# Two k transposes as paired row tiles, and a new order of steps and loads, in an attention and token-MLP kernel

## The chip, the cores and the metric

One core of one Trainium2 chip. The metric is the device time of one execution in microseconds (us). Before: 114.95 us, the median of 3 runs (114.75 to 115.07). The *span* of a run, which the traces show, is about 2 us shorter than its time.

## The reference

Two attentions after each other (32 packed queries p against k and v, then q against what that gives), and on their output a token-mixing MLP with relu:

```python
# batch 8, heads 8, seq 576, head_dim 64, 32 packed queries; float32 in and out
p_packed = softmax_attn(p, k, v)                # (8, 8, 32, 64)
x = softmax_attn(q, p_packed, p_packed)         # (8, 8, 576, 64) -> (8, 576, 512)
W_tok = (1 / 8) * einsum('bsd,btd->bst', x @ w_q, x @ w_k)      # w_q, w_k: (512, 64)
out = relu(einsum('bst,btd->bsd', W_tok, x)) @ w_out            # w_out: (512, 512)
```

## The kernel before

The kernel is written as one long list of steps, `ORDER`, that a loop turns into instructions one by one; no scheduler moves them. `KT.7.0=4` is step KT (transposes of k), batch 7, part 0, into PSUM bank 4; `@A`, `@V` and `@P` name ScalarE (ACT), VectorE (DVE) and GpSimd (POOL). In this kernel a bank has one user at a time: whoever fills it next waits until its last content was copied out.

The steps that matter here: LD loads k, q or v of a batch; KT and QT transpose them and KE and QE copy the result out of PSUM; S1 and PV are the first attention; RS, RR and AM are the sum, reciprocal and product of the second softmax, AT transposes its result; GM, Y and MX are the matmuls of the token mixing, RL its relu, and YE copies the result of Y; OT is the last matmul, OE copies its result into an output buffer, and a full buffer is stored. In the first 26 us, WARM are matmuls whose result nobody uses, and PX transposes p.

```python
opool = ctx.enter_context(tc.tile_pool(name="opool", bufs=9))      # output buffers: nine pairs
psum = ctx.enter_context(tc.tile_pool(name="psum", bufs=1, space=bass.MemoryType.PSUM))

def bank(n, shape, dt, name):
    return psum.tile(shape, dt, tag=f"bank{n}", name=name)

KROW, MROW = (), range(8)              # KROW: the batches with k in row tiles

def KT(b, c, eng, bk):
    if b in KROW and c == 0:           # already there, unused in before
        src = k_in[b].rearrange("a u n -> a (u n)")
        T["kt", b, c] = [bank(n, [P, 16, 64], bf16, "kT_ps") for n in bk]       # two banks
        for n, m in enumerate(KM[0] + KM[1]):
            for i in range(2):         # rows 0-63 and 64-127 in turn
                nc.tensor.transpose(T["kt", b, c][i][:, n], src[halves(i), m * P:(m + 1) * P],
                                    idb[halves(i), halves(i)])
        return
    ...                                # else: 128x128 transposes, eight to a bank

def OE(b, t, *a):                      # copy a result into its half of an output pair
    ...
    o = new("o", (b, tp), [P, 2, D], fp32, "o", opool)
    copy(eng, o[:, t % 2, x:x + w], T["ot", b, t, x])
    done[b, tp] = done.get((b, tp), 0) + w
    if done[b, tp] == 2 * D:
        store(o.rearrange("a e n -> a (e n)"), b, tp * 8, 2)        # two DMAs of 256 KB

def put(dst, o):
    if last: held.append(nc.sync.dma_start(dst, o))
    else:    held.append((dst, o))     # stores are held back ...

def release(load):                     # ... until the last load in ORDER has landed
    last.append(load)
    for n, (dst, o) in enumerate(held):
        i = nc.sync.dma_start(dst, o)
        if n == 0:
            tc.add_manual_dep(i.ins, load.ins.name, ...)            # wait for that load
```

The softmax here doesn't subtract the row's maximum and nothing guards it: scores larger than these inputs give would overflow.

## Time and profile before

| | before |
|---|---|
| median time | 114.95 us |
| span of the profiled run | 112.9 us |
| TensorE busy | 103.7 us (92%) |
| ACT, DVE, POOL busy | 74%, 65%, 34% |
| last load landed | 78.20 us |
| first two stores: issued, landed | 78.29 and 78.99, 81.21 and 81.89 us |
| TensorE's last matmul ends | 107.50 us |

TensorE is busy in nearly every slice. Its share says little about single waits, so the view to start from is the waits of TensorE (line of the waiting instruction, what ended the wait, total us, times, longest us). Three entries are all that before has:

```profile
PE warm_ps L603 <- DVE warm L138: 1.5, 1, 1.5
PE kT_ps L298 <- DMA k_sb<-in_k_dram: 0.9, 1, 0.9
PE pv_ps L340 <- ACT e L328: 0.6, 1, 0.6
```

The first is the start of the program, the last lies at 13.8 us in the first batch. Between them stands the one wait that a change can remove, for k of batch 7. What these lists don't show are instructions that run slowly; for that I use an *offset*: the start of a step in the trace, minus the sum of the undisturbed durations of all matmuls ahead of it in `ORDER`. An offset that stays level means that TensorE runs at its own pace; each step up is a wait or a slow stretch.

### The profile page before, as it was taken

Reading aid. Unit: us, or ns where it says so; the run is one execution under the profiler, and the core shown is the slowest. Engines: PE = TensorE matmul, PEld = TensorE weight load, DVE = VectorE, ACT = ScalarE, POOL = GpSimd, SP = SyncE. Lnnn points to the kernel's source line nnn. Section 1 sums busy time; section 2 is a strip of 40 time slices with the busy share of each in tenths; the row PEclk is TensorE's granted clock in tenths of the full one; section 3 lists DMA queues with packets and bytes.
Section 4 is the critical chain, followed back from the end, with each engine's and each line's share of the span. In section 5 each row is a group of like instructions: output and inputs, shape, how many; then the busy total and the mean of one; then the engine's idle time right before and its main releaser. Section 6 shows DMA issues by size and latency. Waiting matters only on the chain.

```text
span 112.9 us, 4280 instructions
## 1 busy us (share of the span) xinstructions
PE 103.7 (92%) x1842; PEld 73.3 (65%) x1855; DVE 73.5 (65%) x186; ACT 83.0 (74%) x169; POOL 38.3 (34%) x49
## 2 busy tenths in 40 slices
PE   4999799999999999999999999699999999999900
PEld 2458768688767758797848876594985664644500
DVE  2066776947988667795959895669688484916300
ACT  0026859998996875998989676687999989958420
POOL 6972206962550000585490390040008053000000
PEclk9999999999999999999999999999999999999996
DMA  3999999999999999999999999991889999994893
GB/s 83 379 202 206 208 190 209 208 207 211 204 217 203 212 209 211 209 208 211 209 209 209 214 207 208 205 175 26 256 282 312 305 334 338 319 333 148 291 316 135
DMA packets 16035, 25.44 MB, mean 225 GB/s; under 512 B 2656, under 2 KB 10848, under 8 KB 16016
## 3 DMA queue, kind: packets, MB, share of 16 engines
q0 software_dynamic: 11792, 14.42, 73.6%
q1 hardware_dynamic: 3872, 9.90, 26.6%
q10 hardware_dynamic: 352, 0.85, 2.3%
q8 instruction: 14, 0.23, 0.8%
q14 instruction: 5, 0.04, 0.1%
HBM read 30.15 MB, written 9.44 MB: 351 GB/s over the span
## 4 chain that ended last, share of the span: by engine, by line
PE 70%; DMA 12%; ACT 7%; DVE 2%; issue 2%; POOL 1%
PE out_ps L536 22%; DMA k_sb<-in_k_dram 12%; PE warm_ps L603 7%; PE kT_ps L298 6%; PE qT_ps L386 6%; PE pv_ps L340 5%; PE aT_ps L440 4%; PE e_ps L322 4%; PE wkq_ps L461 3%; PE mix_ps L504 3%; PE e_ps L405 3%; ACT kT L131 2%; PE wkq_ps L456 2%; PE g_ps L478 2%; ACT e L414 1%
## 5 line engine op out<-in xcount | busy, mean ns | idle before, releaser
L431 POOL TENSOR_TENSOR a<-e,rr 128x512 bf16<-128x512 f32 (+1 forms) x13 | 16.1, 1245 | 45.1 <-DVE rr L425 21.6
L536 PE MATMUL out_ps<-wout,relu 128*128 128x512 bf16 (+1 forms) x120 | 30.6, 373 | 0.6
L131 ACT ACTIVATE o<-out_ps 128x512 f32<-128x512 f32 (+1 forms) x26 | 15.4, 590 | 7.7 <-PE out_ps L536 7.4
L536 PEld LDWEIGHTS <-relu 128*128 128x128 bf16 x132 | 11.8, 98 | 10.1 <-issue 0.3
L421 DVE TENSOR_REDUCE rs<-e 128x16 f32<-128x512 f32 (+1 forms) x16 | 12.9, 809 | 3.2 <-ACT e L414 3.0
L514 ACT ACTIVATE relu<-mix_ps 128x512 bf16<-128x512 f32 x21 | 11.5, 607 | 1.4 <-PE pv_ps L340 1.2
L414 ACT ACTIVATE e<-e_ps 128x512 f32<-128x512 f32 (+1 forms) x24 | 11.7, 530 | 0.7 <-PE e_ps L405 0.5
L603 PE MATMUL warm_ps<-warm 128*128 128x512 f32 (+1 forms) x24 | 10.8, 580 | 1.5 <-DVE warm L138 1.5
L131 ACT ACTIVATE qT<-qT_ps 128x1024 bf16<-128x1024 bf16 (+1 forms) x12 | 9.8, 831 | 2.4 <-PE qT_ps L386 2.4
L328 ACT ACTIVATE e<-e_ps 128x512 bf16<-128x512 f32 (+1 forms) x24 | 11.2, 502 | 0.2 <-PE e_ps L322 0.2
L386 PE MATMUL qT_ps<-idb,q_sb 128*64 128x128 bf16 x288 | 10.9, 220 | 0.0
L298 PE MATMUL kT_ps<-idb,k_sb 128*128 128x128 bf16 x126 | 9.9, 220 | 0.9 <-DMA k_sb<-in_k_dram 0.9
L386 PEld LDWEIGHTS <-q_sb 128*64 128x64 bf16 x288 | 8.8, 110 | 0.7 <-issue 0.3
L135 DVE COPY kT<-kT_ps 128x1024 bf16<-128x1024 bf16 (+1 forms) x14 | 7.8, 566 | 2.0 <-PE kT_ps L298 2.0
L516 DVE TENSOR_SCALAR relu<-mix_ps 128x512 bf16<-128x512 f32 x11 | 7.3, 687 | 2.6 <-PE mix_ps L504 2.0
L298 PEld LDWEIGHTS <-k_sb 128*128 128x128 bf16 x126 | 7.5, 98 | 2.2 <-DMA k_sb<-in_k_dram 1.1
L340 PE MATMUL pv_ps<-v_sb,e 64*64 64x192 bf16 x288 | 8.4, 244 | 0.6 <-ACT e L328 0.6
L182 POOL DMA_DIRECT2D k_sb<-in_k_dram x7 | 5.3, 761 | 7.6 <-PE ppT_ps L356 3.1
L461 PE MATMUL wkq_ps<-aT,pqk 128*128 128x256 bf16 (+1 forms) x64 | 7.9, 233 | 0.0
L135 DVE COPY o<-out_ps 128x512 f32<-128x512 f32 (+1 forms) x7 | 4.6, 654 | 4.7 <-PE out_ps L536 3.6
L322 PE MATMUL e_ps<-pdiag,kT 128*64 128x64 bf16 x288 | 7.4, 197 | 0.0
L440 PE MATMUL aT_ps<-idb,a 128*128 128x128 bf16 x80 | 7.1, 220 | 0.2
(81 smaller groups left out, 193.3 us busy)
## 6 DMA issues: line engine op xcount, KB each, us to landing
out_dram<-o SPq DMA_DIRECT2D x31, 256.0 KB, 3.8
q_sb<-in_q_dram POOLq DMA_DIRECT2D x8, 576.0 KB, 13.8
v_sb<-in_v_dram POOLq DMA_DIRECT2D x8, 576.0 KB, 12.6
k_sb<-in_k_dram POOLq DMA_DIRECT2D x7, 576.0 KB, 13.0
out_dram<-o_rem SPq DMA_DIRECT2D x4, 256.0 KB, 4.1
k_sb<-in_k_dram ACTq DMA_DIRECT2D x1, 576.0 KB, 3.6
k_sb<-in_k_dram SPq DMA_DIRECT2D x1, 576.0 KB, 5.0
wout<-in_moe_w_out_dram POOLq DMA_DIRECT2D x2, 256.0 KB, 13.0
```

The source lines that it names most:

```text
L131: nc.scalar.activation(o, i, COPY)
L135: nc.vector.tensor_copy(o, i)
L298: nc.tensor.transpose(ps[:, n], src[:, o:o + P], idb if b else idf)
L322: nc.tensor.matmul(ps[halves(i), at[0]:at[1] + 1:at[1] - at[0]], T["kT", b][:, place(b, m), halves(i)], rhs, start=True, stop=True)
L340: nc.tensor.matmul(T["pv", b][i][halves(cc)], lhsT, rhs, start=n == 0, stop=n == R - 1, skip_group_check=True)
L386: nc.tensor.transpose(o[halves(x)], q_in[b][:, x, r * Dh:(r + 1) * Dh], idb)
L414: nc.scalar.activation(e2(b, min(c, 1))[:, o:o + n], T["s2", b, c].rearrange("a t i c (x l) -> a (t i c x) l", l=L), EXP, scale=scale)
L421: e.tensor_reduce(rs, T["e2", (b, d)], axis=AX, op=ADD)
L431: e.tensor_tensor(a2[:, 2 * d:2 * d + n].rearrange("a t i (u l) -> a (t i u) l", l=L), T["e2", (b, d)], T["rr", (b, d)].to_broadcast((P, n ...
L440: nc.tensor.transpose(ps[:, i, t - 2 * c], T["a2", b][:, t, i], idb)
L536: nc.tensor.matmul(ps, lhsT, wout[:, j, x:x + w], start=j == 0, stop=j == NJ - 1)
L603: nc.tensor.matmul(ps[:, 0:n], warm[:, 0:P], warm[:, 0:n], start=True, stop=True)
```

## The change

Two things: k of batches 6 and 7 goes through two row tiles at once (32 transposes of 64 rows in place of 16 of 128), and all steps and loads have a new order. The intent: shorter transposes, and k of batch 7 needed later, so that its load isn't waited for. Nearly all of the diff is `ORDER`; its core:

```diff
-    KROW, MROW = (), range(8)
+    KROW, MROW = (6, 7), range(8)
...                                     # start, loads k7 and k6, end (excerpts)
-LD.p0 LD.K0 LD.K1 LD.p1 LD.P SET.warm@V LD.q0 SET.aT1@V WARM.0=0 SET.idf@V LD.v0 SET.aff@P
-KT.0.0=1 KT.0.1=2 WARM.1=3 PX.0=4 LD.k1 KT.0.3=5 KT.0.4=6 KE.0.0@V KE.0.1@V LD.W SET.pd0@V
+LD.p0 LD.K0 LD.K1 LD.p1 SET.warm@V WARM.5=0 SET.idf@V LD.P WARM.0=1 SET.aff@P PX.0=2 WARM.9=3
+WARM.7=4 SET.pd0@V KT.0.4=5 KT.0.1=6 KE.0.1@A KT.0.3=7 LD.q0 SET.v0@V SET.mask@V KT.0.2=0
...
+KT.6.0=6,0 MR.3=3 PP.5.1@V OT.3.2=2 AE.4.1@V PT.5=5 OT.3.3=4 AE.4.0@A WKQ.4.0=1 OE.3.2@A
...
-KE.7.0@A AE.5.1@V X2.6.1@A KT.7.2=6 WKQ.5.0=5 S2.6.0=1 WKQ.5.1=4 WR.5@V KT.7.1=0 S1.7.0=3 WE.5.0@A
-QT.7.1=2 KE.7.2@V X2.6.0@A QT.7.0=6 X2.6.2@A S1.7.2=5 KE.7.1@V RS.6.0@V RS.6.1@V QT.7.2=1 X1.7.0@A
-WE.5.1@A S1.7.1=7 QE.7.0@A QK.6=0 QKE.6@V GM.5=3 OT.4.1=4 X1.7.1@A GE.5@A Y.5=6 RR.6.0@V X1.7.2@A
+QE.6.1@V AT.5.1=5 AE.5.2@A AE.5.1@V KT.7.0=4,6 PT.6=7 AT.5.0=0 PE.6@V KT.7.1=3 AE.5.0@V KE.7.1@A
+WKQ.5.1=1 WKQ.5.2=2 S2.6.1=5 S2.6.2=7 WKQ.5.0=0 X2.6.2@A OT.4.3=3 MR.4=7 WR.5@V KE.7.0.1@V
+WE.5.0@V WE.5.1@A KE.7.0.0@V X2.6.1@A GM.5=2 S2.6.0=6 OE.4.3@A S1.7.0=1 X2.6.0@A GE.5@V S1.7.2=0
+QK.6=5 QT.7.2=4 QT.7.1=3 RS.6.1@V S1.7.1=2 RS.6.0@V X1.7.2@A X1.7.0@A QKE.6@A QT.7.0=6 Y.5=0
...
```

The loads end, in before, with k6 v5 q6 q7 k7 v6 v7, and after with q6 v5 k6 q7 v6 k7 v7.

## The prediction

Some clauses are cut from it, and marked; none of them is a term of its sum, which comes to 113.8 us, put at 113.7, from durations and offsets in the trace of before.

> **What bounds the kernel now.** I read the page first (engine shares, slices), then the chain of waits in order of time, then TensorE's timeline, then the issues and landings of the loads.
>
> ```profile
> PE 103.7 (92%) x1842; PEld 73.3 (65%) x1855; DVE 73.5 (65%) x186; ACT 83.0 (74%) x169; POOL 38.3 (34%) x49
> PE   4999799999999999999999999699999999999900
> PEclk9999999999999999999999999999999999999996
> DMA  3999999999999999999999999991889999994893
> GB/s 83 379 202 206 208 190 209 208 207 211 204 217 203 212 209 211 209 208 211 209 209 209 214 207 208 205 175 26 256 282 312 305 334 338 319 333 148 291 316 135
> ```
>
> TensorE is full in nearly every slice, at the full clock; the others stand at 34 to 74%. The transfers run at a steady 205 to 215 GB/s up to slice 26 (76 us): these are the loads. From slice 28 on the stores follow, held back by the kernel until the last load has landed. So there are two belts beside each other: TensorE, and the loads. Which leads is seen in the chain and the timeline:
>
> ```profile
> 57.05 1.43 POOL a L431
> 58.48 14.07 DMA k_sb<-in_k_dram
> 72.59 0.62 PE kT_ps L298 x8
> ...
> 105.60 1.91 PE out_ps L536 x12
> 107.53 0.60 ACT o L131
> ```
>
> ```profile
> 50.76 1.03 PE L536 MATMUL out_ps<-wout,relu 128*128 128x512 bf16 x3
> 51.62 0.40 PE L478 MATMUL g_ps<-wkq,a 128*128 128x64 bf16 x8
> 51.85 0.22 PE L478 MATMUL g_ps<-wr,a 128*128 128x64 bf16 x2
> 51.91 1.17 PE L298 MATMUL kT_ps<-idb,k_sb 128*128 128x128 bf16 x18
> 52.92 0.28 PE L405 MATMUL e_ps<-ppT,qT 128*128 128x64 bf16 x4
> ...
> 72.59 0.62 PE L298 MATMUL kT_ps<-idb,k_sb 128*128 128x128 bf16 x8 [0.94 <-DMA k_sb<-in_k_dram]
> 73.14 0.30 PE L488 MATMUL y_ps<-pp,g 64*64 64x128 bf16 x4
> 73.37 0.44 PE L322 MATMUL e_ps<-pdiag,kT 128*64 128x64 bf16 x16
> ```
>
> The 14 us of "DMA" in the chain are k of batch 7, issued at 58.48 and landed at 72.55; all that time TensorE worked on other things, and only 0.94 us of idle TensorE came of it. Its last matmul ends at 107.5, an eviction (0.60) and the last stores make 112.9. From start to start the timeline gives the true rate: 18 transposes in 1.01 us are 56 ns each; the block at 72.59 takes 0.55 where 8 x 56 = 0.45, so a change of tiling mode (128x128 to 64x64) costs about 0.10, and over all such places 0.094.
>
> With such numbers for each kind of step (0.864 for four 512-column matmuls, 29 ns for 64 columns, 15.6 ns for the paired half-array ones of L322, 28 ns for L386, 79 for four of L340) I added up all matmuls in the order of before: 99.35 us. The place of each step in the trace is this sum plus an offset that only waits raise: 1.46 (start), +1.85 (cold first matmuls: the first four take 3.6 us, later ones half), 5.4 at 28 us, 5.9 at 40, 6.4 at 65 (small waits in the first batches, and drift), +1.10 at the k of batch 7, 8.0 at the end. So half the waiting is in the first 26 us, and later there is one wait worth naming.
>
> [...]half-array pairs come 31 ns a pair for 64 columns, and a mode change costs 94 ns. [...]the changed kernel gives each row tile its own bank. [...]before has 29 ns for 64 columns, and 15.6 where two tiles alternate[...]. [...]here all bf16 loads come from POOL on one queue, and before shows them land one by one, one per 2.83 us (589,824 B / 2.83 us = 208 GB/s[...]).
>
> **The change part by part.**
>
> Row tiles. For batches 6 and 7, 16 of 18 transposes of 128x128 become 32 of 64 rows, each moving 64 columns, two alternating in two row tiles and banks. If they pair as L322's column tiles do: 32 x 15.6 = 0.50 us against 16 x 56 = 0.90; 0.40 saved a batch, 0.80 in all. Evictions: still two of 1,024 columns and one of 256 a batch (0.68 on DVE, 1.02 on ACT), but with 64-element runs in the output, and the scores of a batch now need both. They come microseconds later; no cost. Each block adds two changes of mode (4 x 0.094 = 0.38), but the new order saves as many: I counted 56 changes in both kernels. Warm-up matmuls are the same ten. So TensorE's sum falls from 99.35 to 98.55.
>
> Order. k of batch 7 is now wanted much later: 71.1 in the new sum, 65.1 in the old. That wait goes (1.10). But the loads too stand in another order, and k of batch 6 has gone from seventh to fifth of the loads counted from the end. I put the loads in the landing slots of before (k4 46.05, ... v5 63.02, then 66.35, 69.03, 72.55, 75.36, 78.20) and compared with where the new sum wants them. The offset needed so that no step waits: k2 5.2, k3 5.5, q2 5.7, v3 5.9, q3 6.1, v4 6.4, v5 6.3, k6 6.8, k7 only 4.3, v7 1.3. Before's own offset there is 5.2 to 6.4. So the new order runs TensorE right along the belt of loads from 26 to 66 us, and k of batch 6 (slot 66.35, wanted at 59.55 + 6.4 = 65.95) costs some 0.4. After it nothing waits on a load.
>
> Sum. TensorE starts k of batch 6 at 66.4. Left in the new sum: 39.0 (row tiles counted). Drift as in before from there to the end, without the k7 wait: 0.46. For new small waits I add 0.35: near the end all four relus of batch 7 stand on DVE (4 x 0.69 = 2.75 us, against some 2.9 us of matmuls before the first that needs the last of them), and batch 6's y is evicted behind an output copy. That gives 106.2 for the last start, against 107.34: 1.1 us less. The tail (last eviction, last stores, 5.4) is built the same. Stores: after 79.6 us they need about 0.8 us per 256 KB, and before has the queue empty at 102 to 103.5; they can end about a microsecond sooner, hardly two. So span 112.9 - 1.1 = 111.8, and with the 2.05 by which time and span differ, 113.8. A little of the chance lies lower (no wait for k6, no small waits), so I say 113.7.
>
> **The rivals.**
>
> 1. The loads still set the end. For: the slots are tight at k6, and a PE that gains before 66 us gains nothing. Against: the stall needs only 0.4. If q6's slot (3.3 us, a slow one in before) was slow by chance, k6 lands at 65.9 and the time is 113.3. If the loads slip, for instance because POOL issues one late behind a multiply that waits for DVE, as it did at 45 us, each microsecond is one in the end: 114.7.
>
> 2. Row tiles don't pair[...]. Before has no such case; its 48-row transposes in one row tile (33 in 1.25 us with four mode changes) take some 26 ns each. 32 x 26 = 0.83: nearly nothing saved, and the time is 114.4. Only batches 6 and 7, those behind the last tight load, have the change; saving in the earlier ones would gain nothing by the argument above, so this choice fits with a true saving.
>
> 3. The stores bind the end. They need 36 x 0.8 = 28.6 from 79.6, that is 108.2 if never short of data, and the last ones run until 111.5. With TensorE 1.1 sooner there is still slack; with 2 there would not be. This caps the gain at about 2 us, 113.0.
>
> 4. The first batches wait more. The first transposes start later (tally 4.2 against 1.7), but the belt of loads takes up any offset to 6.8, so up to a microsecond costs nothing.
>
> **Range and chances.** The centre is 113.7. Everything well (no k6 wait, no new waits): 112.9. No pairing and half a microsecond of new waits: 114.8. 2% faster is 112.65, and needs more than row tiles, the k7 wait and the k6 slot together give: 0.08. 2% slower is 117.25 and needs a stall of 3 us that nothing points to: 0.02. Within 2%: 0.90.
>
> **What would show it.** Right: the transposes of L298 in batches 6 and 7 start 15 to 16 ns apart, 0.50 us a block; no wait of TensorE for k of batch 7; a wait of 0.2 to 0.6 for k of batch 6 near 66 us; landings still 2.83 apart and the last near 78.2; TensorE's end near 106.3; the tail 5.4. Wrong: starts 25 ns apart or more; the last load later than 79; waits of TensorE for ACT or DVE of over 0.5 us in the last 40 us; store slices full up to the end with the last eviction long done.

## The result, and the profile after

After: 116.65 us, the median of 4 runs (116.31 to 118.25); before in the same rounds 114.92 (114.75 to 115.07). The ratio of the fast runs is 1.0141, with a 95% interval of 1.011 to 1.0172. Ratios here are the mean time of one kernel's fast runs over the mean of the other's of the same rounds, so not quite the ratio of the medians. Executions over 1.5% slower than the fastest of the same kernel are left out of the means. I had predicted 113.7 with 112.9 to 114.8: a gain of 1.2 us where there is a loss of 1.7.

The profiled run was a slow one (118.25 us), so what follows is checked below in a fast one. The page's slices, engine TensorE and moved GB/s:

```profile
PE   4999999999999999999999979999969997999800
GB/s 85 375 201 205 188 212 207 209 207 208 210 209 206 209 213 210 210 211 208 213 205 208 215 203 210 206 85 50 206 310 321 307 334 344 302 201 289 287 266 87
```

From 14 us on, TensorE's slices were full in before but for one (the wait for k of batch 7); now one at 66 us, one at 84 and one at 95 are not. The waits of TensorE name all three:

```profile
PE qT_ps L386 <- ACT o L131: 1.2, 1, 1.2
PE kT_ps L290 <- DMA k_sb<-in_k_dram: 0.7, 1, 0.7
PE aT_ps L440 <- POOL a L431: 0.4, 1, 0.4
PE aT_ps L440 <- DVE a L431: 0.2, 1, 0.2
```

And TensorE's timeline (start us, busy us, line, tiles, shapes, count, and in brackets the idle time and what ended it):

```profile
67.08 0.64 PE L290 MATMUL kT_ps<-idb,k_sb 64*128 64x64 bf16 x32 [0.66 <-DMA k_sb<-in_k_dram]
67.65 0.29 PE L509 MATMUL mr_ps<-wr,y 128*128 128x128 bf16 x2
...
80.97 1.03 PE L536 MATMUL out_ps<-wout,relu 128*128 128x512 bf16 x4
...
84.52 0.64 PE L386 MATMUL qT_ps<-idb,q_sb 128*64 128x128 bf16 x16 [1.16 <-ACT o L131]
...
96.19 0.40 PE L440 MATMUL aT_ps<-idb,a 128*128 128x128 bf16 x4 [0.40 <-POOL a L431]
```

The row tiles do as predicted: 67.08 to 67.65 is 0.57 us, of which one mode change takes 0.094 (as in before); 32 transposes in 0.48 are 15 ns each, against 0.90 us for the sixteen of before. The wait for k of batch 7 is gone. But the step at 84.52, QT.7.1, waits 1.16 us for an output copy on ACT. That copy is OE.4.3, of the bank that the OT at 80.97 had begun to fill 3.5 us before. Why it came so late is in the chain of waits (start us, us, what):

```profile
75.79 2.71 PE out_ps L536 x12
78.52 0.60 ACT o L131
79.44 4.33 DMA out_dram<-o
83.88 0.60 ACT o L131
84.52 0.64 PE qT_ps L386 x16
```

and ACT's timeline shows the copy itself waiting for a store:

```profile
83.88 0.60 ACT L131 ACTIVATE o<-out_ps 128x512 f32<-128x512 f32 x1 [1.72 <-DMA out_dram<-o]
```

Read from the bottom: QT.7.1 needs bank 3; bank 3 is free when OE.4.3 has copied it out; OE.4.3 opens the *tenth* output pair (batch 4, tiles 2 and 3), and there are nine buffers; so it waits for the first pair to be stored; no store may start until the last load has landed (78.66), so the first two were issued at 78.74 and 79.44, and they landed at 83.16 and 83.77. In before the tenth pair's first copy came later: OT.4.1 of the tenth pair came on TensorE at 84.5, its copy at 85.3, without a wait, and the first pair had landed at 81.89. From before's timelines of TensorE and ACT:

```profile
84.47 0.81 PE L536 MATMUL out_ps<-wout,relu 128*128 128x512 bf16 x3
85.32 0.60 ACT L131 ACTIVATE o<-out_ps 128x512 f32<-128x512 f32 x1
```

There is a second part: these stores took 4.4 us where those of before took 2.9. The trace of the DMA packets shows a cause by its time, not by name. One instruction transfer of 16 KB (the profile's queue 8, "instruction") runs from 80.0 to 81.7 us, and right behind it the stores stand nearly still. This is the DMA view of 78 to 86 us, in slices of 0.2 us; the four low ones are 81.8 to 82.6 us:

```profile
GB/s 0 0 0 0 0 0 0 0 0 0 287 225 143 246 328 369 307 287 307 62 20 20 20 184 225 225 205 369 410 348 307 379 348 379 399 256 184 266 184 287
```

In three of the four 20 GB/s flow, against 287 to 369 in the microsecond before. What holds the stores there is not shown.

In before that transfer came at 82.2, when two stores had landed and the third was about to (82.66); the fourth took 5.2 us. Part of that is its place in the queue: in a later run of before's order (k of batch 7 loaded earlier) the transfer came only at 83.9, and the fourth store took 3.9 us without it.

Where the time went, in offsets (us) at five places. The fast run is the first experiment below:

| offset of TensorE at | predicted | after (slow run) | after (fast run) |
|---|---|---|---|
| the row tiles of batch 6 | 6.8 | 7.5 | 7.4 |
| 84 us, before QT.7.1 | | 7.7 | 7.5 |
| 88 us | | 9.4 | 9.3 |
| 98 us, behind AT.7 and MX.6 | | 10.4 | 10.3 |
| the end | 7.6 | 10.4 | 10.4 |
| last matmul ends | 106.3 us | 109.12 us | 109.11 us |

The sum of matmuls is 98.55 us in all three columns. The end is 2.8 us later than predicted and the time 2.95 us longer.

### The profile page after: what moved, and what is told of

Same layout as the page of the kernel before. It is cut to its first block, busy times and chain, and to the rows that moved or that the text cites. A ratio compares the mean times of both kernels' runs of the same rounds, so it can differ in the third digit from the quotient of the medians.

```text
span 115.2 us, 4349 instructions
## 1 busy us (share of the span) xinstructions
PE 104.9 (91%) x1887; PEld 72.6 (63%) x1887; DVE 81.2 (70%) x200; ACT 75.0 (65%) x158; POOL 34.5 (30%) x46
## 4 chain that ended last, share of the span: by engine, by line
PE 67%; DMA 13%; ACT 7%; DVE 4%; issue 3%; POOLq 1%; POOL 0%; SPq 0%; ACTq 0%; DVEq 0%
PE out_ps L536 20%; PE warm_ps L603 9%; DMA k_sb<-in_k_dram 9%; PE kT_ps L298 6%; PE qT_ps L386 5%; PE pv_ps L340 5%; DMA out_dram<-o 4%; PE e_ps L322 4%; PE e_ps L405 3%; PE mix_ps L504 2%; PE wkq_ps L461 2%; PE aT_ps L440 2%; ACT o L131 2%; ACT relu L514 1%; DVE rs L421 1%
## 5 line engine op out<-in xcount | busy, mean ns | idle before, releaser
L431 POOL TENSOR_TENSOR a<-e,rr 128x512 bf16<-128x512 f32 (+1 forms) x10 | 12.3, 1237 | 51.0 <-DVE rr L425 24.5
L131 ACT ACTIVATE o<-out_ps 128x512 f32<-128x512 f32 (+1 forms) x30 | 17.8, 595 | 11.6 <-PE out_ps L536 9.2
L536 PEld LDWEIGHTS <-relu 128*128 128x128 bf16 x132 | 11.5, 98 | 11.3 <-issue 1.9
L603 PE MATMUL warm_ps<-warm 128*128 128x256 f32 (+1 forms) x24 | 11.6, 611 | 1.5 <-DVE warm L138 1.5
L516 DVE TENSOR_SCALAR relu<-mix_ps 128x512 bf16<-128x512 f32 x17 | 11.2, 681 | 1.0 <-PE mix_ps L504 0.9
L514 ACT ACTIVATE relu<-mix_ps 128x512 bf16<-128x512 f32 x15 | 8.1, 596 | 3.7 <-issue 1.4
L131 ACT ACTIVATE kT<-kT_ps 128x256 bf16<-128x256 bf16 (+2 forms) x7 | 4.5, 638 | 7.3 <-PE kT_ps L298 7.3
L135 DVE COPY qT<-qT_ps 128x1024 bf16<-128x1024 bf16 (+1 forms) x14 | 8.2, 589 | 1.2 <-PE qT_ps L386 1.2
L135 DVE COPY aT<-aT_ps 128x512 bf16<-128x512 bf16 (+1 forms) x17 | 5.9, 357 | 3.0 <-PE aT_ps L440 3.0
L298 PE MATMUL kT_ps<-idb,k_sb 128*128 128x128 bf16 x94 | 7.4, 219 | 0.0
L322 PEld LDWEIGHTS <-kT 128*64 128x64 bf16 x288 | 6.4, 112 | 1.5 <-DVE rr L425 0.8
```

The source lines that it names most:

```text
L131: nc.scalar.activation(o, i, COPY)
L135: nc.vector.tensor_copy(o, i)
L298: nc.tensor.transpose(ps[:, n], src[:, o:o + P], idb if b else idf)
L322: nc.tensor.matmul(ps[halves(i), at[0]:at[1] + 1:at[1] - at[0]], T["kT", b][:, place(b, m), halves(i)], rhs, start=True, stop=True)
L431: e.tensor_tensor(a2[:, 2 * d:2 * d + n].rearrange("a t i (u l) -> a (t i u) l", l=L), T["e2", (b, d)], T["rr", (b, d)].to_broadcast((P, n ...
L536: nc.tensor.matmul(ps, lhsT, wout[:, j, x:x + w], start=j == 0, stop=j == NJ - 1)
```

## The experiments

Sixteen kernels, all correct. Kernels of one heading group ran on the same chip beside the same runs of before: 115.45 us (median of 11 runs) for the first four (chip 3), 115.08 for the second (chip 9), 115.15 for the third (chip 2) and 114.99 for the last (chip 9 again). The theory from the traces (A): nine output buffers are too few for this order, and the copy of the tenth pair waits for the first stores. Rivals: B, the wait belongs to the slow profiled run; C, the loss is in the stores' rate, whoever waits; D, the row tiles themselves harm.

### First four: the unchanged kernel, the buffers, the release, the row tiles

**The changed kernel again.** No edit.

> The changed kernel once more, unaltered, for a profile in the usual state (the first one was 118.25 us against 116.3 to 116.8 of its fast runs). Theory A (a tenth output pair finds no free output buffer, because all stores wait for the last load): ACT again waits about 1.5 us on the landing of a store ahead of an output copy near 82 us, and TensorE over 1 us for it. Rival B (that wait belongs to the slow profile only): no such wait, and the fast time of 116.5 comes from elsewhere. Time 116.2 to 116.9 either way.

Measured: 116.60 us, ratio 1.0118 (1.0075 to 1.016), and the profile fell in a fast run. The waits of TensorE in it (further entries left out):

```profile
PE qT_ps L386 <- ACT o L131: 1.3, 1, 1.3
...
PE aT_ps L440 <- POOL a L431: 0.4, 1, 0.4
```

The first two stores landed 4.28 and 4.19 us after issue, and an instruction transfer stood at 80.0 us. B falls.

**Ten output buffers.** The room comes from a second pool.

```diff
-    opool = ctx.enter_context(tc.tile_pool(name="opool", bufs=9))
+    opool = ctx.enter_context(tc.tile_pool(name="opool", bufs=10))
-            o = opool.tile([P, D], fp32, tag="orem", name="o_rem", bufs=4)
+            o = opool.tile([P, D], fp32, tag="orem", name="o_rem", bufs=2)
```

> The changed kernel with ten output buffers instead of nine (the room comes from the remainder buffers, two instead of four). Theory A: ACT's wait on a store near 82 us is gone, TensorE's 1.2 us wait behind it too; and if the two later waits (0.3 and 0.6 us near 95 us, for the attention weights of batch 7) are its followers, those as well: 114.3 to 115.3. Rival C (the stores' belt sets the end whatever TensorE does): TensorE ends sooner but the time stays at 116.2 or more. Rival B: no change, 116.5.

Measured: 115.25 us, ratio 0.9987 (0.9942 to 1.0032). The two longest waits of TensorE behind its start:

```profile
PE aT_ps L440 <- POOL a L431: 0.4, 1, 0.4
PE px_ps L257 <- DMA p<-in_p_dram: 0.3, 1, 0.3
```

The wait at QT.7.1 is gone, and the offset after 84 us rises by 0.2 in place of 1.8. The stores are nearly as slow as without the edit (4.03 us, an instruction transfer at 79.8): it is the buffer that makes their slowness matter. The time falls by 1.35 us against the changed kernel on the same chip. TensorE's end is at 107.00. A is confirmed, and it isn't the whole miss: the kernel is now level with before, not 1.2 us faster, and 0.9 us of waits at AT.7 and MX.6 stay.

**Nine buffers, stores released when k of batch 7 has landed.** One load earlier.

```diff
-        end = [item for item in ORDER.split() if item.startswith("LD.")][-1]
+        end = "LD.k7"
```

> The changed kernel with the stores let go when k of batch 7 has landed, one load (2.8 us) before the last. Theory A: the first pair's stores land near 81 us instead of 83.8, the tenth pair finds its buffer, TensorE's wait near 83 us is gone: 114.5 to 115.5, and the tail may gain as the stores start earlier. Rival C: the stores' belt sets the end, and starting it 2.8 us earlier gains nearly that: 113.5 to 114.5, below what ten buffers give. Against both: the stores slow the last load; v of batch 7 is wanted at 85.9 us and has slack of 7.

Measured: 115.44 us, ratio 0.9997 (0.9953 to 1.004). The first stores are issued at 74.94 and land at 78.78; the wait at QT.7.1 is gone too, and TensorE ends at 107.00, as with ten buffers. An earlier start of all stores gains nothing beyond the freed buffer, so nothing speaks for C.

**The new order without row tiles.** Three transposing steps of k in batches 6 and 7 as in before, in the places of the new order.

```diff
-    KROW, MROW = (6, 7), range(8)
+    KROW, MROW = (), range(8)
-KT.6.0=6,0 MR.3=3 ... KT.6.1=6 ...
+KT.6.0=6 KT.6.1=0 MR.3=3 ... KT.6.2=6 ...
-... KT.7.0=4,6 PT.6=7 ... KT.7.1=3 ...
+... KT.7.0=4 KT.7.1=6 PT.6=7 ... KT.7.2=3 ...
```

> The changed kernel's order with the k of batches 6 and 7 transposed as before (18 full transposes, no row tiles). TensorE's sum rises by 0.8 us less two pairs of mode changes of 0.19 each, so 0.4. If that lies on the path behind the k of batch 6: 116.9. If theory A holds and part of TensorE's saving is eaten by the wait for the buffer near 82 us (which ends when the store lands, not when TensorE comes), only the batch 7 half counts: 116.6 to 116.8. If row tiles harm (second eviction needed before the scores): below 116.4.

Measured: 115.84 us, ratio 1.0052 (1.0003 to 1.0101): 0.8 us faster than with the row tiles by the medians, though the runs overlap (115.25 to 116.90 against 116.39 to 117.53). The first stores landed 2.91 us after issue (78.01 to 80.92), the instruction transfer came at 82.3, and TensorE had no wait at QT.7.1, still with nine buffers (shorter waits and those of the first batch left out):

```profile
PE kT_ps L298 <- DMA k_sb<-in_k_dram: 0.5, 1, 0.5
PE aT_ps L440 <- POOL a L431: 0.4, 1, 0.4
```

So row tiles and wait are tied together, and not through TensorE's own time, which the row tiles shorten, nor through the harm that the expectation names (D, a second copy before the scores): in the fast run with row tiles no wait of TensorE for the copies KE is listed. They add 64 TensorE instructions (each transpose with its weights is two), and with them the instruction transfer falls 2.3 us earlier, on the first stores. That is theory F, tested later. Without it the second store would land at 79.44 + 2.9 = 82.3, worked out from the 2.9 us of this run; the copy takes 0.6, and QT.7.1 was due at 83.36, where the step ahead of it ended in the changed kernel. The order by itself has only some 0.4 us of slack there, against 2.6 in before between the landing of the first pair and the tenth pair's first matmul.

### Second four: before's order, and the instruction transfers

**Row tiles in before's order.** With KROW = (6, 7); the two banks were found by moving some steps:

```diff
-WR.3@V X2.4.1@A KT.6.2=1 ... KT.6.1=6 WE.3.1@A      (and KT.6.0=5 later)
+WR.3@V X2.4.1@A KT.6.1=1 ... WE.3.1@A               (and KT.6.0=5,3 behind OT.3.2)
-KE.7.0@A AE.5.1@V X2.6.1@A KT.7.2=6 WKQ.5.0=5 ...
+KE.7.1@A AE.5.1@V X2.6.1@A KT.7.0=6,0 WKQ.5.0=5 KE.7.0.0@V KE.7.0.1@V ...
```

> The kernel before, its order and loads kept, with the row tiles for the k of batches 6 and 7 alone (a few steps next to them moved, so that banks are free). Each block saves 0.40 us and adds two mode changes of 0.094: 0.21 less a batch. What batch 6 saves lies ahead of the wait for the k of batch 7 and is lost in it; so about 0.2 us faster than before, ratio 0.998 (0.995 to 1.002). If row tiles as such do harm, which the run of the new order without them (ratio 1.005 against 1.012 with them) could be read as: ratio 1.004 or more.

Measured: 117.27 us, ratio 1.019 (1.0145 to 1.0235), a clear miss. My placement made waits of its own, some 2.3 us by the offsets: the two copies of each block stand on DVE ahead of others, and steps behind them wait (Y twice for the copy of g, 0.4 us each). Another 0.5 us, a wait for q of the first batch at 11.5 us, has nothing to do with it. It says that row tiles, as written here, need two free banks and two copies at once, and that the new order is what makes room for them; about their own worth it says nothing.

**Warm-up matmuls in pieces of 128 columns.** Same work, 96 TensorE instructions more at the start, to move the instruction transfer.

```diff
-                for o in range(0, WARM[int(f[1])], 512):
-                    n = min(512, WARM[int(f[1])] - o)
+                for o in range(0, WARM[int(f[1])], 128):
+                    n = 128
```

> The changed kernel with its warm-up matmuls cut into pieces of 128 columns: the same columns, but 96 more TensorE instructions in the first 21 us. In the traces a 16 KB instruction transfer starts when TensorE's recorded count is near 3,050 (80.0 us with the row tiles, 82.3 without them), and in the changed kernel it falls on the first stores, which land 4.3 us after their issue instead of 2.9. Theory F (that transfer makes the tenth output pair wait): with 96 more instructions it comes near 77 us, ahead of the stores; the first pair lands before 82.3, ACT's wait on a store is under 0.5 us, TensorE's 1.3 us wait is gone; time as with ten buffers, ratio to before 0.997 to 1.003. Rival G (the first stores are late for another reason, such as the last load's landing at 78.7): the waits stay, ratio 1.010 to 1.015.

Measured: 118.79 us, ratio 1.0224 (1.0142 to 1.0306), of only two fast runs. A miss: the transfer still came at 79.7. The first two stores took 3.15 and 3.64 us all the same, less than in the changed kernel, and TensorE, 3.0 us behind by then, had no wait at QT.7.1. While loads run, these transfers come one per 6 us (at 47.5, 53.5, 59.4 and 65.4 in one of the runs below). In before they start 5.6 to 6.6 us apart from 14.6 to 82.2 us, and between two of them TensorE starts 121 to 352 recorded instructions (matmuls and weight loads). In the present run TensorE has waits for which the profile shows no cause, which it calls "issue" (before and the fast run of the changed kernel list none):

```profile
PE warm_ps L603 <- issue: 0.9, 1, 0.9
PE out_ps L536 <- issue: 0.8, 1, 0.8
...
PE pv_ps L340 <- issue: 0.6, 1, 0.6
```

These are 2.3 us. That TensorE ran out of instructions there is my guess and not shown; if it did, that is a third belt beside TensorE and the loads, which I hadn't seen at all, and the 96 added instructions were not free even though their columns were the same.

**Before with k of batch 7 loaded earlier** (its load and that of q of batch 7 exchanged).

```diff
-X1.5.1@A OE.2.3@A OT.2.0=4 LD.q7 AT.3.0=0 ...
+X1.5.1@A OE.2.3@A OT.2.0=4 LD.k7 AT.3.0=0 ...
-GM.3=7 QT.5.2=5 RS.4.1@V LD.k7 OE.2.1@A ...
+GM.3=7 QT.5.2=5 RS.4.1@V LD.q7 OE.2.1@A ...
```

> The kernel before with one thing changed: the loads of k and q of batch 7 change places, so that k lands near 69.5 us instead of 72.55. If the 1.1 us wait of TensorE there is on the path, as the prediction has it: 1.0 us faster, ratio 0.989 to 0.992. Rival (another wait takes its place at once: the stores' belt, or output buffers): ratio 0.995 to 1.0.

Measured: 115.33 us, ratio 1.004 (0.9996 to 1.0084): a miss again. The wait for k is gone, yet nothing is gained. In the profiled run TensorE reached full speed 2.2 us later than in the profile of before (at 7.3 in place of 5.1 us; the eight 128x128 float32 transposes at 5.03 us took 1.71 us to the next start, in before 0.92), which put it 1.1 us behind, and one new wait stood at 86.3 us:

```profile
PE pv_ps L340 <- issue: 0.4, 1, 0.4
```

With k of batch 7 early, the offset at 74 us was 7.6, as in before. In this run, then, the late start used up what the missing wait gave. The wait of 1.10 us that I had put on the list of gains takes up earlier delays as well as making one; without it they run through. Whether that is also why the five runs without a profile gained nothing is not shown.

**The same with the row tiles** of the first kernel of this group added to it (the same lines).

> The same early k of batch 7, with the row tiles of batches 6 and 7 in the order of before. No wait for a load is left that could eat what they save: a further 0.4 us, ratio 0.985 to 0.989. If the 64 added TensorE instructions bring an instruction transfer onto the first stores again: ACT or DVE waits on a store near 84 us, and the ratio is that of the run before it or worse.

Measured: 116.73 us, ratio 1.0145 (1.011 to 1.0179), with the same waits of my placement. Inconclusive for the same reason.

### Third four: the other waits, and all mended

**Ten buffers, and the softmax of batch 7 in another order**: the half that the first AT.7 needs is summed first and multiplied on POOL, the other on DVE.

```diff
-... RS.7.0@V WKQ.6.1=1 RS.7.1@V OT.4.2=0 OT.5.2=3 RR.7.1@V WE.6.1@A RR.7.0@V
-GM.6=4 AM.7.1@V ... AM.7.0@P AT.7.2=1 ...
+... RS.7.1@V WKQ.6.1=1 RR.7.1@V AM.7.1@P RS.7.0@V OT.4.2=0 OT.5.2=3 WE.6.1@A RR.7.0@V
+GM.6=4 AM.7.0@V ... AT.7.2=1 ...
```

> The changed kernel with ten output buffers, and with the softmax sums of batch 7 in another order: the half that the first AT.7 needs is summed first and multiplied on POOL, the other half on DVE. If the waits at AT.7 and MX.6 (0.33 + 0.58 us, unchanged in every run of this order so far) come only from the order of these DVE and POOL steps, they go: TensorE ends near 106.1 and the ratio to before is 0.990 to 0.993. Rival: another wait takes their place (the copies and relus behind them on DVE and ACT move too), and the ratio stays at 0.998, as with ten buffers alone.

Measured: 115.36 us, ratio 1.0008 (0.9965 to 1.0051). In the trace the step did what it should: both waits at AT.7 and MX.6 are gone, and from 69 us to the end the offset rises by 0.5 in place of the 1.4 of ten buffers alone. The time did not follow, and the profile shows something new. In it, and in the three that follow, TensorE stood at half speed until 10.6 us (128x128 float32 transposes 0.21 us apart, 0.11 later), where all earlier profiles had left it between 4.4 and 7.3. At 69 us the offset was 8.4 in place of 6.9.

**Row tiles in batch 6 only**, nine buffers, otherwise the changed kernel.

```diff
-    KROW, MROW = (6, 7), range(8)
+    KROW, MROW = (6,), range(8)
-... KT.7.0=4,6 PT.6=7 ... KT.7.1=3 ... KE.7.1@A ... KE.7.0.1@V ... KE.7.0.0@V ...
+... KT.7.0=4 KT.7.1=6 PT.6=7 ... KT.7.2=3 ... KE.7.2@A ... KE.7.1@V ... KE.7.0@V ...
```

> The changed kernel with row tiles in batch 6 only: 32 TensorE instructions fewer, nothing else moved, still nine output buffers. Theory F (the instruction transfer that falls on the first stores makes the wait at QT.7.1): that transfer comes about 1 us later than in the changed kernel, 81 or later, the first two stores land 2.9 to 3.4 us after issue, the wait at QT.7.1 is 0.4 us or less, and the ratio is 1.002 to 1.006. Rival G (the wait belongs to the order, whatever the instruction transfer does): the wait stays above 0.9 us and the ratio is 1.011 or more.

Measured: 116.39 us, ratio 1.0098 (1.0061 to 1.0135). In the profiled run the transfer came at 82.2, the first stores landed in 2.93 us and there was no wait at QT.7.1, all as F says; but with the late start TensorE came to this step 1.1 us later than in the fast run of the changed kernel, which alone would have hidden most of the wait. Undecided, and the ratio is outside what I expected of F.

**All mended**: ten buffers, the softmax order, release at k of batch 7, and k of batch 6 loaded before q of batch 6.

```diff
-LD.q6 WR.2@V ...
+LD.k6 WR.2@V ...
-... PV.4.2 LD.k6 ...
+... PV.4.2 LD.q6 ...
-        end = [item for item in ORDER.split() if item.startswith("LD.")][-1]
+        end = "LD.k7"
```

> The changed kernel with ten output buffers, the softmax order of the run above, k of batch 6 loaded before q of batch 6, and the stores released when k of batch 7 has landed. If the causes found add up (wait at QT.7.1 and its follower 1.6, AT.7 and MX.6 0.9, k of batch 6 0.3 to 0.7), the ratio is 0.985 to 0.990, the fastest so far. Rival: TensorE's instruction supply or the loads take part of it back, 0.993 to 0.998.

Measured: 114.61 us, ratio 0.9948 (0.9905 to 0.999): faster than both kernels, and less than expected: it lies in the range named for the rival, but what was taken back is not shown. Of the six runs, the profiled one has a span of 113.4 with the late start, the others 112.0 to 113.2.

**The same without row tiles.**

```diff
-    KROW, MROW = (6, 7), range(8)
+    KROW, MROW = (), range(8)
```

> The same kernel as the one above without the row tiles, so that nothing but these differ where no wait hides it. By the prediction's own working a row-tile block saves 0.40 us of transposes, of which the two changes of tiling mode that it brings (2 x 0.094) take 0.19: this kernel should be 0.42 us slower, a ratio 0.003 to 0.005 above that of the run above. Rival: the 64 more instructions of the row tiles cost as much in TensorE's instruction supply as they save, and the two ratios are equal within 0.002.

Measured: 114.51 us, ratio 0.9929 (0.9888 to 0.997). Two of its runs, the profiled one with its late start among them, were called slow (spans 114.0 and 114.5) and are not in the ratio, where the run above with the same late start was called fast; so the two ratios don't compare. Both profiles have the late start: TensorE ends at 107.56 with row tiles and 108.07 without.

### Last four: the start

In the late profiles TensorE's warm-up matmuls were followed by nine small transposes of p (32x32) at 6.02 us, and then by more warm-up. TensorE's timeline in the all-mended kernel's profile:

```profile
1.46 4.63 PE L603 MATMUL warm_ps<-warm 128*128 128x256 f32 x6 [1.46 <-DVE warm L138]
6.02 1.16 PE L257 MATMUL px_ps<-idf,p 32*128 32x32 f32 x9
```

The speed changed at 10.6 in all four late profiles; what sets that time, no run here shows. Theory H: the new order's warm-up, with the transposes in its middle, makes a late start possible (a guess of mine). The edit puts them behind the warm-up (a "solid start" below):

```diff
-... WARM.0=1 SET.aff@P PX.0=2 WARM.9=3
-WARM.7=4 SET.pd0@V ...
+... WARM.0=1 SET.aff@P WARM.9=3
+WARM.7=4 PX.0=2 SET.pd0@V ...
```

**All mended, with it.**

> The all-mended kernel with one TensorE step moved: the first nine small transposes (of p, 32x32) come after the warm-up matmuls, not between them. In the four profiles of the last call TensorE left half speed only at 10.5 us[...], while in all earlier profiles it left it between 4.7 and 7.0. Theory H: in the new order those small transposes lie in the warm-up[...], so some runs start 2 us later. Then [...]the six timed spans stand together (112.0 to 112.8) and the ratio is 0.988 to 0.992. Rival: the late start is the chip's or the run's, whatever the warm-up holds; then some spans are still 113 or more and the ratio stays at 0.995.

Measured: 114.44 us, ratio 0.9966 (0.9913 to 1.0019). Full speed came at 6.5 us (and at 7.4, 7.6 and 6.0 in the three that follow):

```profile
1.46 6.20 PE L603 MATMUL warm_ps<-warm 128*128 128x256 f32 x10 [1.46 <-DVE warm L138]
7.58 0.74 PE L257 MATMUL px_ps<-idf,p 32*128 32x32 f32 x9
```

The six spans are 111.8 to 112.4, close together as expected (mean 112.10, before 112.97 on the same chip, 0.8% more). The times are not: two runs took 115.27 and 115.30 with spans of 112.1 and 111.9, so 3.2 and 3.4 us lie outside the span, where it is 2.0 to 2.4 in the others. What was expected of the spans held within 0.2 us (112.0 to 112.8), what was expected of the ratio didn't.

Theory H is not shown by this. All four late profiles come from chip 2, and all four with the edit from chip 9; the new order with the old warm-up left half speed by 4.9 us in all four profiles on chip 3. That the late start belongs to the chip stays a rival: no profile has the edit on chip 2, or the late start elsewhere.

**The same without row tiles** (KROW empty, as above).

> The same kernel as the one above without the row tiles. With equal starts the worth of the row tiles is what lies between the two: 0.42 us expected (a ratio 0.003 to 0.005 above that of the run above); in the last pair TensorE's end differed by 0.51 us, but the times were spread by the starts. Rival: equal within 0.001.

Measured: 114.32 us, ratio 0.9949 (0.9908 to 0.9989); spans 112.1 to 112.9, mean 112.40. By the times it is the faster, by the spans the slower by 0.3 us; neither difference is outside the spread. TensorE ends at 106.24 with row tiles and 106.53 without. That the row tiles save 0.42 us of TensorE's sum is measured; that this reaches the time is not shown.

**The changed kernel, with it.**

> The changed kernel with nothing but the small transposes moved behind the warm-up. If the late start had a share in the changed kernel's loss, it gets faster: 1.002 to 1.007. If the wait for the output buffers rules, whose end is fixed by the stores and takes up whatever TensorE gains before it, nothing is gained: the wait at QT.7.1 is 1.1 to 1.5 us and the ratio 1.010 to 1.014. I expect the second.

Measured: 116.56 us, ratio 1.011 (1.0059 to 1.0161), where the changed kernel had 1.0118. The offset rises by 1.46 at QT.7.1 (its profile fell in a slow run; the first store took 4.57 us, the transfer came at 79.6):

```profile
PE qT_ps L386 <- ACT o L131: 1.3, 1, 1.3
```

So the late start, which the changed kernel's own two profiles don't have either, has no visible share in the loss: the wait for the stores ends at a time that TensorE doesn't set, and takes up what TensorE gains before it.

**Row tiles in batch 6 only, with it.**

> Row tiles in batch 6 only, with the small transposes moved likewise: the run that failed to decide on theory F (the instruction transfer on the first stores makes the wait at QT.7.1), because its late start hid the wait. With an early start, theory F: that transfer starts at 81 us or later, the first stores land in 2.9 to 3.4 us, the wait at QT.7.1 is at most 0.4, the ratio 1.001 to 1.006. Rival G (the wait belongs to the order with nine buffers, whatever the transfer does): wait 0.9 or more, ratio 1.010 or more.

Measured: 115.99 us, ratio 1.0081 (1.0036 to 1.0126). A miss in what it was built for: the transfer did not come at 81 or later but at 79.5. With that, the first stores took 4.03 and 3.95 us and the wait is there, if shorter. TensorE's waits:

```profile
PE qT_ps L386 <- ACT o L131: 0.7, 1, 0.7
```

and in the waits of ACT:

```profile
ACT o L131 <- DMA out_dram<-o: 1.5, 2, 1.3
```

So what F says of the *effect* (first stores of 4 us or more and a wait at QT.7.1 where a transfer falls on them, 2.9 us and no wait where none does) held in five of the six kernels of the new order with nine buffers and release at the last load; the exception is the warm-up in pieces. What it says of the *cause*, that 32 instructions fewer move the transfer by a microsecond, did not. Side by side, with the changed kernel in its fast run (late start only in the fourth row):

| kernel (nine buffers) | transfer starts | first store takes | offset step at QT.7.1 |
|---|---|---|---|
| changed, fast run | 80.0 | 4.28 us | 1.44 |
| changed, solid start | 79.6 | 4.57 us | 1.46 |
| row tiles in batch 6, solid start | 79.5 | 4.03 us | 0.88 |
| row tiles in batch 6, late start | 82.2 | 2.93 us | none |
| no row tiles | 82.3 | 2.91 us | none |
| changed, warm-up in pieces | 79.7 | 3.15 us | none |

In the two kernels of the new order without row tiles and with earlier release it stood at 83.5 and 82.6, in those with row tiles at 81.2 and 80.3. So in each of the three pairs of the new order that differ in the row tiles of both batches alone, the transfer comes 2.3 us earlier with them (in before's order, where my placement made TensorE late, it came at 82.2 with and without). The traces point to a count: when it began, TensorE had started 3,008 to 3,107 recorded instructions in 17 of the 18 profiles (3,195 in the other). With the row tiles that count is reached earlier, but 50 instructions either way are 1.2 to 1.4 us at the 42.0 (before) and 34.7 (after) recorded instructions per us between 75 and 85 us, and what sets the exact time stays open.

## Why the prediction was wrong

- **The wait for k of batch 7**: right, it goes. But booking its whole length as gain was wrong: in before with k loaded early, 1.10 us of wait went and the time did not fall.
- **Row tiles**: right. 15 ns each, 0.48 us a block, 0.80 us off the sum (98.55), and equal mode changes.
- **The wait for k of batch 6**: predicted 0.2 to 0.6; the offset rises there by 0.7 (slow run) and 0.3 (fast run). But its load came at 67.03 and 66.90 us, not in the slot of 66.35 that I had taken over from before, so the offset behind it was 7.4, not 6.8; this term was 0.6 too small.
- **Small new waits, 0.35**: the term that failed. It measured 2.7 us: 1.8 from QT.7.1 with the OT.4.1 behind it, and 0.9 at AT.7 and MX.6. The second of these lies where I looked (the end of batch 7), but I had looked at the relus and the y copy; the softmax products on POOL and DVE were what came late. The first I didn't see.
- **The step "Stores"**, and with it rival 3, is where it should have been seen. I reckoned the stores as a rate (0.8 us per 256 KB; at the 305 to 338 GB/s of slices 30 to 35 of before it is 0.78 to 0.86) that ends early enough, and asked whether they bind the *end*. I did not count output buffers: nine pairs, all held until the last load lands, and the tenth pair moved from 85 to 82 us in the new order. And I did not ask how long one store takes to land: before has 2.9 us for its first three, and 5.2 for the fourth.
- **Drift**: predicted 0.46, about 0.26.
- **The tail**: right, 5.4 predicted, 5.5 in the fast run.
- **Two slips** that change nothing: 36 stores of 0.8 us are 28.8 us, not the 28.6 of rival 3; and 107.34 is the sum with its offset, where the last matmul in the trace of before starts at 107.12.
- **The signs of being wrong**: one of them came, a wait of TensorE for ACT of over 0.5 us in the last 40 us (1.16 and 1.28 us at QT.7.1).

Summed over the fast run's offsets: +0.6 at k of batch 6, +1.8 at QT.7.1, +0.9 against 0.35 at AT.7 and MX.6, -0.2 of drift, together +2.8, which is the measured delay of TensorE's end. My chance of 0.02 for a stall of 3 us "that nothing points to" was the consequence: something did, in the number of buffers. "Within 2%" held by luck, with the wrong sign; of the gain of 1.1 us only the shorter sum of matmuls was real.

What the experiments show of the cause: the buffer wait is shown; ten buffers take 1.35 us off and an earlier release 1.16, and on that chip the changed kernel was 1.15 us slower than before. The softmax wait is shown in the trace. What that wait is worth in time is not shown: with ten buffers and the other softmax order TensorE gained 0.9 us behind 69 us, in a run that started 1.5 us late. That the instruction transfer makes the stores late rests on coincidence in the profiles, with one exception among the nine-buffer kernels, not on a run that moved the transfer at will.

## What to carry to other kernels

When an order moves, count the buffers: for each pool, find which use first needs a buffer given back, when it now comes, and what gives it back; a store that is held on purpose is a deadline for all who share its buffers. A wait at which several delays meet may be worth less than its length: ask what it absorbs before you book it as gain. And look at what added instructions bring with them: 96 more for the same columns came with 2.3 us of waits here for which the profile shows no cause.
